# Row gathers, row sizes and weight preparation re-placed in the block stage of a Fourier layer, an expert layer and a SoLU layer

## The chip, the cores and the metric

One core of one Trainium2 chip runs the whole program in one launch. The metric is device time in microseconds (us), the median of several executions. Engines by their names in the profile: PE (matmul), ACT, DVE and POOL (elementwise work; POOL also issues the row gathers, the row scatters and some weight loads), SP (issues the other transfers).

## The reference, cut to what matters

Three layers in a row, all in float32:

```python
X = rfft(x, axis=1)                      # x: 8 x 3072 x 256
Yr, Yi = softshrink(Xr@w_r - Xi@w_i + b_r), softshrink(Xr@w_i + Xi@w_r + b_i)   # lam 0.01
x = irfft(Yr + 1j*Yi).reshape(24576, 256)

e = argmax(x @ w_gate); gate = softmax(x @ w_gate)[e]      # 8 experts
# the first 768 rows of each expert, in row order, are kept; the others give zero rows
y = gate * (relu(x @ w1[e]) @ w2[e])                        # 256 -> 1024 -> 256

h = y @ w_in                                                # 256 -> 1024
s = h * softmax(h)
out = ((s - mean(s)) / sqrt(var(s) + 1e-6) * g_ln) @ w_out  # 1024 -> 256
```

With these inputs every expert has its 768 rows within the first 3 of the 8 batches, so the kernel transforms 3 batches and runs the rest only if a count says otherwise (a branch at the end that is not taken here).

## The kernel before, in words

**Three batches, then sixteen blocks.** Each batch passes a Fourier stage in 12 units (the loop `units`, which calls `middle(u)` after each unit) and an inverse stage (`tail`) that stores rows to `ydram` in HBM and writes down, for every expert, which rows it keeps. Then each expert's 768 places are worked off as 2 blocks of 384 rows (3 tiles of 128 rows), in the order of experts 0, 1, 1, 0, 2, 2, 3, 3, ... 7, 7. I number these blocks 0 to 15. Two slots hold an expert's prepared weights, one for the even experts and one for the odd ones.

**One block.** *gather* (L830): POOL issues 3 indirect DMAs that fetch 3 x 128 rows into one of two row buffers. *words* (L834 to L849): ACT squares each row tile with a sum (L841), DVE makes a power-of-two scale of it (L842, L786 to L788), ACT and DVE split the rows into a high and a low float16 part (L846, L847), and SP issues one DMA transpose of them (L848). *up* U0 to U3 (L873): 12 matmuls each, relu on ACT (L875) and the low part on DVE (L876). *down* D0 to D3 (L888 to L891): 12 matmuls each, which need the relu of the up of the same number. *finish* F (L900 to L909). Then, mixed into the next block: *hidden* H0 to H2 (L925 to L966), one per row tile, with the second layer's first matmul, an exponential (L934) and moments; *norm* N (L972 to L977, on POOL); *halves* C (L965 to L967), which end in a DMA transpose on SP; and *project* P or Q (L996 to L999) with 24 matmuls that need that transpose and an indirect store to `out` on POOL.

**An expert's weights.** `expert_steps` returns steps: four chunks of 512 KB are fetched (L648, L650; chunks 0 and 1 on POOL's queue, 2 and 3 on SP's, in the block stage), each chunk is squared and summed on ACT (`size`, L653, 1.2 us), a pair of sums is added by two one-column matmuls on PE (L659) and made a scale (`scale`), and each half chunk is split on ACT (L674, 0.7 us) and DVE (L675, 0.75 us) (`part`). The second layer's first weight has the same in `first_steps` (L736, L739, L747, L748). Chunks 2 and 3 are the second half of the expert's weights, which the down matmuls read.

**What sets the order.** `run_blocks` writes the program of each block from a list of letters: `ORDER_0` for block 0, `ORDER_1` for block 1, `ORDER` for the others. G is the gather of the next block, X its *words*, E takes the next weight step of the list `side[n]` of this block; steps left over after the last letter follow behind F. What is written is not yet what runs: a planner of the framework lays out each engine's queue from its own estimate of times. It takes an instruction as soon as the inputs and the buffer are there by its estimate, and of several the one that was written first; each engine then runs its queue strictly in that order. The only fences are `pinned()` and `issue_after`: every weight step E is queued behind the last ACT and the last DVE instruction written before it, and `PIN_X = (2,)` does that to the *words* written in block 2 (those of block 3).

**Weight steps before.** 11 steps: all four fetches; two squares and their scale; two squares and their scale; 8 parts. For an expert whose first block is n, the first 5 stand in block n-2 and, after an empty one, 6 in block n-1, which has 5 letters E (so two parts fall behind F). For expert 2 all 11 stand in block 3. Expert 0's own steps are taken in the last batch's units 6 to 11, two a unit, and the 5 steps of `first_steps` (four squares with their matmuls, then 4 parts) in units 7 and 8.

Of the kernel before, what the change touches and what calls it, by code (L numbers as in the profile page):

```python
# [30 lines left out]
GATHER = 9  # L31


ORDER_0 = 'E R U0 L E R U1 E R E D0 R U2 E R E E R D1 E R U3 E R D2 R G E X D3 E E F'.split()

DRAIN = 'I0 I1 S0 M0 I2 B1 T0 S1 M1 B2 T1 S2 M2 T2 P0 P2 P1'.split()
LATER = 8
PIN_X = (2,)
ORDER_1 = 'E U0 H0 U1 D0 E H1 N0 U2 E D1 C0 E G H2 N1 U3 C1 P0 E N2 C2 X D2 D3 F'.split()
BEHIND = ()  # L40
ORDER = 'E Q1 U0 H0 D0 G U1 E Q2 N0 H1 D1 U2 E C0 E H2 N1 C1 X U3 D2 P0 E N2 C2 D3 F'.split()
ROUTE = ((-2, -6), (-2, -6), (-2, -5))
NCH = 8
COUNT = 3
# [83 lines left out]
def _body(tc, x, w_r, w_i, b_r, b_i, w_gate, w1, w2, w_in, w_out, g_ln, cap, con, out):  # L128
# [15 lines left out]
    with sp as sb, dp as dr, pp as ps:  # L144
# [495 lines left out]
        def expert_steps(e, o, load=(dma,) * 4):  # L640

            flat = lambda c: v(o_st + 1024 * c, 1024)
            squares = v(o_flag + 4, 4)

            def fetch(c):
                k = c % 2
                if c < 2:
                    load[c](out=flat(c), in_=w1[bass.ds(e, 1), 128 * k : 128 * k + 128, :].rearrange("o p f -> (o p) f"))  # L648
                else:
                    load[c](out=v3(o_st + 1024 * c, 4, D), in_=w2[bass.ds(e, 1), 512 * k : 512 * k + 512, :].rearrange("o (c p) d -> (o p) c d", p=128))  # L650

            def size(c):
                act(v(o_xr + 1536, 1024), flat(c), ACTF.Square, accum_out=squares[:, c : c + 1])  # L653

            def scale(m):
                p = psum("psc")
                for k in range(2):
                    c = 2 * m + k
                    mm(p[:, 0:1], ones16, squares[:, c : c + 1].bitcast(BF16)[:, 1:2], start=k == 0, stop=k == 1)  # L659
                total = squares[:, 2 * m : 2 * m + 1]  # L660
                vec.tensor_scalar(total, p[:, 0:1], 1e-36, None, ALU.max)
                scales(*weight_scales(o)[m], total, 10)

            def part(c, r):
                h1, l1, h2, l2 = expert_views(o)
                k = c % 2
                if c < 2:
                    at = slice(512 * r, 512 * r + 512)
                    h, l, src = h1[:, k, at], l1[:, k, at], flat(c)[:, at]
                else:  # L670
                    at = slice(4 * k + 2 * r, 4 * k + 2 * r + 2)
                    h, l, src = h2[:, at], l2[:, at], v3(o_st + 1024 * c, 4, D)[:, 2 * r : 2 * r + 2]
                w = weight_scales(o)[c // 2][0]
                act(h, src, ACTF.Copy, scale=w)  # L674
                vec.scalar_tensor_tensor(l, src, w, h, ALU.mult, ALU.subtract)  # L675

            def load_all():
                for c in range(4):
                    fetch(c)

            def half_sized(m):
                size(2 * m)
                size(2 * m + 1)
                scale(m)

            return [load_all] + [lambda m=m: half_sized(m) for m in range(2)] + [lambda c=c, r=r: part(c, r) for c in range(4) for r in range(2)]

        behind = []

# [40 lines left out]
        def first_steps():  # L730

            part_of = lambda a, n: a[:, n // 2, 512 * (n % 2) : 512 * (n % 2) + 512]

            def size():
                for n in range(4):
                    act(v(o_xr, 512), part_of(wi, n), ACTF.Square, accum_out=v(o_flag + 4 + n, 1))  # L736
                p = psum("psc")
                for n in range(4):
                    mm(p[:, 0:1], ones16, v(o_flag + 4 + n, 1).bitcast(BF16)[:, 1:2], start=n == 0, stop=n == 3)  # L739
                total = v(o_flag + 4, 1)  # L740
                vec.tensor_scalar(total, p[:, 0:1], 1e-36, None, ALU.max)
                scales(*i_scale, total, 10)
                vec.tensor_scalar(i_scale[1], i_scale[1], float(2**DOWN), None, ALU.mult)

            def part(n):
                h, l, src = part_of(wi_h, n), part_of(wi_l, n), part_of(wi, n)
                act(h, src, ACTF.Copy, scale=i_scale[0])  # L747
                vec.scalar_tensor_tensor(l, src, i_scale[0], h, ALU.mult, ALU.subtract)  # L748

            return [size] + [lambda n=n: part(n) for n in range(4)]  # L750

        o_w16 = (o_wsb, o_ht + 5120)
        last_weights = lambda: tuple(v(o, 1024).bitcast(F16).rearrange("p (f d) -> p f d", f=8) for o in o_w16)
# [47 lines left out]
        class Block:  # L801
# [23 lines left out]
            def gather(self):  # L825
# [3 lines left out]
                for i in range(NTT):  # L829
                    pool.indirect_dma_start(out=v(o_xg + D * (NTT * self.par + i), D), out_offset=None, in_=ydram[0 : self.rows, :],  # L830
                                            in_offset=bass.IndirectOffsetOnAxis(ap=self.slots(i, 0), axis=0),
                                            bounds_check=self.rows - 1, oob_is_err=False)

            def words(self):  # L834

                at = o_sx + 16 * self.par
                square, power, back = (v(at + 4 * i, NTT) for i in range(3))
                a = f16(o_xr + 768 * self.par, 4).rearrange("p (h k) (i c) -> p h i k c", h=2, i=NTT)
                rows = [v(o_xg + D * (NTT * self.par + i), D) for i in range(NTT)]
                for i in range(NTT):  # L840
                    act(v(o_xr + 2560, D), rows[i], ACTF.Square, accum_out=square[:, i : i + 1])  # L841
                vec.tensor_scalar(square, square, 1e-36, None, ALU.max)  # L842
                scales(power, back, square, 6)
                for i in range(NTT):
                    src, s = rows[i].rearrange("p (k c) -> p k c", k=2), power[:, i : i + 1]
                    act(a[:, 0, i], src, ACTF.Copy, scale=s)  # L846
                    vec.scalar_tensor_tensor(a[:, 1, i], src, s, a[:, 0, i], ALU.mult, ALU.subtract)  # L847
                dma(out=f16(o_ga + 768 * self.par, 4).rearrange("p a (i c) -> p (a i) c", c=128),  # L848
                    in_=v(o_xr + 768 * self.par, 768).bitcast(F16), transpose=True)  # L849
# [199 lines left out]
        def in_order(strict):  # L1049
            return pinned() if strict else ExitStack()  # L1050
# [80 lines left out]
        def run_blocks(blocks, side, free=None, marks=()):  # L1131
# [8 lines left out]
            for n in range(len(blocks)):  # L1140
# [11 lines left out]
                for what in (ORDER_0, ORDER_1, ORDER)[min(n, 2)]:  # L1152
                    i = int(what[1:] or 0)
                    if what[0] == "E":
                        extra()
                    elif what[0] == "U":
                        bl("up")(i)
                    elif what[0] == "D":
                        bl("down")(i)
                    elif what[0] == "R":  # L1160
                        if n == 0 and marks:
                            marks.pop(0)()
                    elif what[0] == "G":
                        of(n + 1, "gather")()
                    elif what[0] == "H":
                        pr("hidden")(i)
                    elif what[0] == "N":
                        if n > 0 and i in BEHIND:
                            with tc.issue_after(blocks[n - 1].exped):
                                pr("norm")(i)  # L1170
                        else:
                            pr("norm")(i)
                    elif what[0] == "C":
                        pr("halves")(i)
                    elif what[0] == "P" and not late:
                        pr("project")(i)
                    elif what[0] == "Q":
                        of(n - 2, "project")(i)
                    elif what[0] == "X":
                        with in_order(n in PIN_X):  # L1180
                            of(n + 1, "words")()
                    elif what[0] == "F":
                        bl("finish")()
                        if late:
                            pr("project")(0)
# [44 lines left out]
        blocks = [Block(e, e * capp + k * BLK, n, where[e], rows, own=n if n < 2 else None) for n, (e, k, rows) in enumerate(plan)]  # L1230
        side = {n: [] for n in range(len(plan))}
        for i, e in enumerate(rest):
            owner = ([EARLY[1], EARLY[0]] + rest)[i]
            first = max(n for n, o in enumerate(order) if o == owner) + 1
            steps = expert_steps(e, where[e], [pool.dma_start] * 2 + [dma] * 2)
            if first + 1 < order.index(e):
                side[first] += steps[:5]
                side[first + 1] += [lambda: None] + steps[5:]
            else:
                side[first] += steps  # L1240

        early = expert_steps(EARLY[0], slot_a)
        load_c2(0, 8)
# [26 lines left out]
        for b in range(FIRST):  # L1270
# [32 lines left out]
            def before_last(b=b, last=last, steps=steps):  # L1303
# [2 lines left out]
                renew(o_hn)  # L1306
                if last:
                    renew(o_ga)
                    blocks[0].words()
                    sums.extend(column_sums())  # L1310
                    sums.pop(0)()
                else:
                    begin(x[b + 1])
# [40 lines left out]
        with tc.If(more > 0):  # L1354
# [24 lines left out]
            with tc.For_i(0, NE, 1) as e:  # L1379
# [5 lines left out]
                    vec.tensor_copy(dst.bitcast(I32) if f < 2 else dst, src[:, bass.ds(e * n, n)])  # L1385
                again = [Block(e, 0, k, slot_a, NT, False, k) for k in range(nblk)]
                again[0].gather()
                again[0].words()
                renew(o_hn)
                run_blocks(again, {})  # L1390
# [26 lines left out]
```

## Time and profile before

| what | value |
|---|---|
| median of 3 runs | 948.74 us (947.61 to 949.88) |
| the profiled execution's own time | 949.85 us |
| its span, first to last instruction | 948.0 us |
| PE busy | 847.8 us (89%) |
| DVE, ACT, POOL busy | 638.2, 481.9, 287.7 us |
| mean granted PE clock | 0.956 |

A busy PE is one with a matmul in its pipeline; at half the clock the same matmuls look twice as long. The idle time in front of an instruction is printed in brackets, with what ended it. The first block's F stands at 358.3 us, the last one's at 913.2 us. All times within the trace are counted from the span's start.

### The profile page before, as it was taken

To read this page: it belongs to the slowest core of one execution; us is meant where nothing else is said; L and a number is where in the kernel's file an instruction comes from. 1 tells how busy PE (TensorE), PEld (TensorE's weight loads), DVE (VectorE), ACT (ScalarE), POOL (GpSimd) and SP (SyncE) were. 2 spreads that over 40 slices of the span, in tenths; PEclk is the share of its full clock that TensorE was granted. 3 is DMA by queue.
4 is the path that set the end of the run, shared out by engine and by line. 5 is a ranking of instruction groups with operands and counts; after the bars stand their busy time and mean duration, and the time that the engine had idled before them with its cause. 6 is when DMAs were issued, how large, how long until landed. Compare 5 with 4: busy or idle time off the path is not lost. (4 is left out here: it accounts for less than half of the span.)

```text
span 948.0 us, 16083 instructions
## 1 busy us (share of the span) xinstructions
PE 847.8 (89%) x5844; PEld 571.4 (60%) x5844; DVE 638.2 (67%) x1640; ACT 481.9 (51%) x848; POOL 287.7 (30%) x450
## 2 busy tenths in 40 slices
PE   8799999999978999796887979788798898899996
PEld 3797479945967465563544645455455565566656
DVE  1475589757976678584765857466575786687674
ACT  2343344333474547375755656365465664565443
POOL 2000000000002044546445344452444434334435
PEclk9899999999979999997989999889898999999999
DMA  8899659975993421534364253362544445432330
GB/s 225 283 287 287 207 165 286 285 249 174 294 301 94 119 81 60 109 84 104 80 151 112 49 136 78 79 148 46 112 83 112 95 80 133 74 67 63 56 79 32
DMA packets 211273, 131.74 MB, mean 139 GB/s; under 512 B 126390, under 2 KB 193331, under 8 KB 211056
## 3 DMA queue, kind: packets, MB, share of 16 engines
q1 hardware_dynamic: 204448, 110.91, 45.9%
q0 software_dynamic: 6736, 19.71, 7.3%
q8 instruction: 48, 0.79, 0.3%
q14 instruction: 41, 0.34, 0.1%
HBM read 50.37 MB, written 50.33 MB: 106 GB/s over the span
## 5 line engine op out<-in xcount | busy, mean ns | idle before, releaser
L996 PE MATMUL pso<-r,r 128*128 128x256 f16 (+1 forms) x792 | 145.1, 286 | 23.0 <-DMA r<-r 22.5
L873 PE MATMUL psH<-r,r 128*128 128x384 f16 x768 | 139.1, 332 | 0.7 <-DVE r L675 0.5
L996 PEld LDWEIGHTS <-r 128*128 128x128 f16 x1080 | 108.7, 102 | 48.4 <-DMA r<-r 26.8
L433 PE MATMUL psm<-r,r 128*128 128x256 f32 x864 | 116.0, 291 | 5.1 <-DVE r L404 3.5
L433 PEld LDWEIGHTS psm<-r,r 128*128 128x128 f32 x864 | 108.8, 196 | 6.1 <-DVE r L404 3.9
L873 PEld LDWEIGHTS <-r 128*128 128x128 f16 x768 | 76.2, 100 | 54.8 <-issue 4.8
L942 DVE SCALAR_TENSOR_TENSOR r<-psh,r 128x1024 f32<-128x1024 f32 x48 | 58.8, 1224 | 48.6 <-ACT r L934 48.4
L888 PE MATMUL psY<-r,r 128*128 128x384 f16 x256 | 55.3, 340 | 40.3 <-ACT r L875 40.3
L830 POOL DMA_INDIRECT r<-ydram,r x48 | 55.3, 1151 | 108.9 <-DVE r L615 61.3
L996 PE MATMUL pso<-r 128*128 128x256 f16 x360 | 87.9, 287 | 0.0
L891 PE MATMUL psY<-r,r 128*128 128x384 f16 x256 | 86.0, 337 | 1.0 <-DVE r L876 0.9
L972 POOL TENSOR_SCALAR r<-r 128x1 f32<-128x1 f32 x48 | 16.2, 338 | 231.6 <-ACT r L952 173.0
L890 PE MATMUL psY<-r,r 128*128 128x384 f16 x256 | 86.3, 338 | 0.0
L875 ACT ACTIVATE r<-psH 128x768 f16<-128x768 f32 x64 | 51.5, 805 | 67.7 <-PE psH L873 65.2
L934 ACT ACTIVATE r<-psh,r 128x1024 f32<-128x1024 f32 x36 | 43.3, 1202 | 69.6 <-DVE r L933 38.9
L876 DVE SCALAR_TENSOR_TENSOR r<-psH,r 128x768 f16<-128x768 f32 x64 | 61.0, 954 | 18.0 <-ACT r L875 17.3
L926 PE MATMUL psh<-r,r 128*128 128x512 f16 x192 | 72.7, 379 | 0.0
L925 PE MATMUL psh<-r,r 128*128 128x512 f16 x192 | 72.7, 379 | 0.0
L932 DVE TENSOR_REDUCE r<-psh 128x1 f32<-128x1024 f32 x48 | 58.5, 1219 | 14.5 <-PE psh L928 14.2
L999 POOL DMA_INDIRECT out<-r x48 | 54.2, 1128 | 31.5 <-DVE r L998 17.9
L966 DVE SCALAR_TENSOR_TENSOR r<-r 128x1024 f16<-128x1024 f32 x36 | 47.6, 1321 | 24.0 <-ACT r L965 22.8
L518 POOL DMA_DIRECT2D r<-c_tok x3 | 1.8, 601 | 200.9 <-DVE r L556 200.4
(212 smaller groups left out, 1663.0 us busy)
## 6 DMA issues: line engine op xcount, KB each, us to landing
out<-r SPq DMA_DIRECT2D x48, 512.0 KB, 6.1
r<-moe_w SPq DMA_DIRECT2D x20, 512.0 KB, 5.0
r<-x SPq DMA_DIRECT2D x24, 384.0 KB, 8.0
r<-gdram SPq DMA_DIRECT2D x36, 256.0 KB, 5.3
ydram<-r SPq DMA_DIRECT2D x36, 192.0 KB, 2.2
r<-moe_w POOLq DMA_DIRECT2D x12, 512.0 KB
gdram<-r SPq DMA_DIRECT2D x12, 384.0 KB, 3.4
ydram<-r SPq DMA_DIRECT2D x36, 64.0 KB, 2.4
```

What stands on the lines that cost most here:

```text
L433: mm(p3[:, gi], a, b, start=i == 0, stop=i == len(seq) - 1)
L830: pool.indirect_dma_start(out=v(o_xg + D * (NTT * self.par + i), D), out_offset=None, in_=ydram[0 : self.rows, :], in_offset=bass.Indirect ...
L873: mm(p3[:, fi, 0:BLK], a, b, start=i == 0, stop=i == 5)
L876: vec.scalar_tensor_tensor(hl_, p3[:, :, 0:BLK], 0.0, hh, ALU.max, ALU.subtract)
L888: mm(y3[:, d, 0:BLK], b, hh[:, fi], start=f == 0, stop=False)
L890: mm(y3[:, d, 0:BLK], a, hh[:, fi], start=False, stop=False)
L891: mm(y3[:, d, 0:BLK], a, hl_[:, fi], start=False, stop=f == 7)
L925: mm(o, a, r, start=k == 0, stop=False)
L926: mm(o, a, w, start=False, stop=False)
L932: vec.tensor_reduce(c(0), p, AX.X, ALU.max, negate=True)
L942: vec.scalar_tensor_tensor(t, p, 1.0, e, ALU.mult, ALU.mult, accum_out=c(3))
L996: mm(p[:, 0:D], a, b, start=n == 0, stop=n == 23)
```

## The change

*words* becomes two functions: `sizes` (the squares and scales, letter X) and `words` (split and transpose, letter Z). A letter K writes the gather for the block after next. `PIN_X` goes. In `ORDER` G is gone and K stands behind P0; X moves from behind C1 to behind U1, and Z stands behind D1. In `ORDER_1` G moves ahead of U2, X behind U3, Z behind C2, and K stands ahead of F. An expert's steps are regrouped into ten (below), five in block n-2 and five in block n-1, for all experts alike. `first_steps` becomes 12 steps: two pairs of squares, three empty steps, the matmuls with the scale, two empty steps, 4 parts; its sums move to places of their own.

```diff
-ORDER_1 = 'E U0 H0 U1 D0 E H1 N0 U2 E D1 C0 E G H2 N1 U3 C1 P0 E N2 C2 X D2 D3 F'.split()
+ORDER_1 = 'E U0 H0 U1 D0 E H1 N0 G U2 E D1 C0 E H2 N1 U3 X C1 P0 E N2 C2 Z D2 D3 K F'.split()
-ORDER = 'E Q1 U0 H0 D0 G U1 E Q2 N0 H1 D1 U2 E C0 E H2 N1 C1 X U3 D2 P0 E N2 C2 D3 F'.split()
+ORDER = 'E Q1 U0 H0 D0 U1 X E Q2 N0 H1 D1 Z U2 E C0 E H2 N1 C1 U3 D2 P0 K E N2 C2 D3 F'.split()
-PIN_X = (2,)
...
-            return [load_all] + [lambda m=m: half_sized(m) for m in range(2)] + [lambda c=c, r=r: part(c, r) for c in range(4) for r in range(2)]
+            groups = [[lambda: fetch(0), lambda: fetch(1)], [lambda: fetch(2), lambda: fetch(3)], [lambda: size(0)], [lambda: size(1)], [lambda: size(2)],
+                      [lambda: scale(0), lambda: size(3)], parts[0:2], [lambda: scale(1), parts[2]], parts[3:6], parts[6:8]]
...
-            return [size] + [lambda n=n: part(n) for n in range(4)]
+            return [lambda: squared(0), lambda: squared(2), wait, wait, wait, size, wait, wait] + [lambda n=n: part(n) for n in range(4)]
...
                     elif what[0] == "X":
-                        with in_order(n in PIN_X):
-                            of(n + 1, "words")()
+                        of(n + 1, "sizes")()
+                    elif what[0] == "Z":
+                        of(n + 1, "words")()
+                    elif what[0] == "K":
+                        of(n + 2, "gather")()
...
+            at = order.index(e)
+            side[at - 2] += steps[:5]
+            side[at - 1] += steps[5:]
```

The arithmetic, the buffers and the counts of instructions of every kind stay as they were.

## Rows read from the trace of the kernel before

**Rows 1.** Busy time per stretch: PE, PEld, DVE, ACT, POOL, clock, DMA.

```profile
589.00:633.30 44.30, 35.09 (x210) 21.52 (x211) 26.36 (x71) 21.34 (x37) 22.69 (x35) 0.89 0.47 107
633.30:670.00 36.70, 33.51 (x205) 20.29 (x204) 25.59 (x71) 22.39 (x40) 11.37 (x17) 0.95 0.40 79
...
854.10:884.10 30.00, 30.00 (x195) 18.85 (x194) 22.31 (x55) 15.86 (x23) 13.16 (x24) 1.00 0.32 67
```

**Rows 2.** Waits from 400 us on: who waited for what, total, times, longest.

```profile
ACT r L841 <- DMA r<-ydram,r: 56.1, 17, 8.1
...
PE psY L888 <- ACT r L875: 40.3, 16, 9.1
...
PE pso L996 <- DMA r<-r: 17.5, 10, 4.3
```

**Rows 3.** ACT in order of time at block 5's start, idle in brackets.

```profile
511.61 0.40 ACT L841 ACTIVATE r<-r 128x256 f32<-128x256 f32 x1
...
519.75 0.42 ACT L841 ACTIVATE r<-r 128x256 f32<-128x256 f32 x1 [7.64 <-DMA r<-ydram,r]
...
520.70 0.79 ACT L875 ACTIVATE r<-psH 128x768 f16<-128x768 f32 x1
```

**Rows 4.** POOL in order of time, same start, then one block later.

```profile
508.45 1.16 POOL L830 DMA_INDIRECT r<-ydram,r  x1 [5.96 <-DVE r L908]
...
513.01 0.63 POOL L648 DMA_DIRECT2D r<-moe_w  x1
...
516.64 1.09 POOL L830 DMA_INDIRECT r<-ydram,r  x1 [0.17 <-issue]
...
542.28 0.65 POOL L648 DMA_DIRECT2D r<-moe_w  x1
```

**Rows 5.** PE in order of time: idle before the first down, and before a project.

```profile
443.54 1.44 PE L888 MATMUL psY<-r,r 128*128 128x384 f16 x4 [9.08 <-ACT r L875]
...
632.15 0.39 PE L996 MATMUL pso<-r,r 128*128 128x256 f16 x1 [4.32 <-DMA r<-r]
...
682.45 1.44 PE L888 MATMUL psY<-r,r 128*128 128x384 f16 x4 [5.18 <-ACT r L875]
```

**Rows 6.** Busy time per stretch around eight waits: first, last, sum.

```profile
434.00:449.50 15.50, 6.42 (x28) 3.56 (x27) 6.16 (x24) 9.77 (x24) 9.12 (x11) 0.67 0.22 62
...
706.00:719.00 13.00, 9.47 (x54) 6.38 (x52) 8.31 (x22) 6.31 (x13) 8.39 (x10) 0.74 0.85 187
sum 94.00, PE 55.35 PEld 32.27 DVE 42.20 ACT 42.47 POOL 46.65; mean PE 6.92 PEld 4.03 DVE 5.27 ACT 5.31 POOL 5.83
```

**Rows 7.** The gathers' and the row squares' lines: first and last start.

```profile
L830 POOL DMA_INDIRECT r<-ydram,r x48: 994/1098/1952, 286.9 to 714.8; - x48
...
L841 ACT ACTIVATE r<-r x48: 399/416/418, 290.6 to 721.0; 128x256 f32<-128x256 f32 x48
```

**Rows 8.** SP in order of time: two transposes of one block.

```profile
532.27 1.79 SPq L967 DMA_TRANSPOSE r<-r  x1
...
542.15 5.39 SPq L967 DMA_TRANSPOSE r<-r  x1
```

**Rows 9.** Busy time per stretch in the last batch, and in block 0.

```profile
262.50:277.80 15.30, 8.96 (x62) 7.93 (x60) 12.19 (x35) 12.71 (x30) 0.00 (x0) 0.80 1.08 321
271.50:282.00 10.50, 7.05 (x35) 6.71 (x35) 7.31 (x22) 9.42 (x20) 0.00 (x0) 0.51 0.89 275
329.80:341.00 11.20, 8.33 (x48) 5.56 (x49) 7.92 (x28) 6.55 (x12) 3.78 (x7) 0.85 0.24 73
```

**Rows 10.** PE in order of time: waits behind weight sizes.

```profile
270.73 0.16 PE L739 MATMUL psc<-r 128*128 128x1 bf16 x1 [1.49 <-ACT r L736]
...
334.85 0.16 PE L659 MATMUL psc<-r 128*128 128x1 bf16 x1 [1.93 <-ACT r L653]
...
657.90 0.81 PE L888 MATMUL psY<-r,r 128*128 128x384 f16 x4 [1.64 <-ACT r L875]
```

**Rows 11.** ACT in order of time: its longest idle time in block 2.

```profile
396.33 0.81 ACT L875 ACTIVATE r<-psH 128x768 f16<-128x768 f32 x1 [7.74 <-PE psH L873]
```

## The prediction on record

> **What bounds the kernel now.** I read the busy time per stretch first. PE is the engine that everything ends on, and in the block stage it runs in two ways. Two neighbouring blocks with weight steps and gathers took 44.3 and 36.7 us, with PE busy 35.1 and 33.5 us of that at a clock of 0.89 and 0.95. A late block without either took 30.0 us with PE busy throughout at 1.00 [rows 1]. The work on PE is the same, so a pair loses some 18 us. DVE is busy 26.4 of 44.3 us, so it is not the bound, nor would it be at 33 us a block (80%).
>
> The waits come second. PE's idle time from 400 us on is nearly all in two lines: 40.3 us in 16 waits of a down matmul for a relu on ACT, and 17.5 us of a project matmul for a transposed half. ACT itself idles 56.1 us in front of the row squares, for gathered rows [rows 2]. The time order shows why these belong together: at block 5's start ACT takes one row square, sits 7.64 us until the next tile has landed, and only then does the relu of U0 [rows 3]. That tile's gather is not waiting for memory: POOL issues the first at 508.45, the third at 516.64, with norm, a scatter and a 512 KB weight fetch in between [rows 4]. PE pays with 9.08 us at 443.54, 5.18 at 682.45 and three like them between (3.49, 4.71, 4.89), 27.4 us in all; three project waits of up to 4.32 us make 11.3 more [rows 5]. Each also costs clock: in the eight stretches around them 0.67 to 0.82 of the pulses were granted, that is at 1.2 GHz for part of the time after the idle, 25.6 us of pulses lost in 94 us. PE was busy 55.4 of these 94, so I count 15 of the 25.6 as lost work [rows 6].
>
> The fact that decides most is in the lines' first and last starts. The last gather, for block 15, is issued at 714.8 and its squares run at 721.0 [rows 7]; block 10 starts there and block 15 some 170 us later. So the planner already runs gathers five to six blocks ahead of use, limited by the two row buffers, wherever the letter G stands.
>
> **Gathers, K, G, X and Z.** No instruction is added or removed: 48 gathers (1.10 us each [rows 7]) and 48 squares stay. In the steady state a row buffer is free when an earlier block's *words* have been read out, and that is set by U3 of the running block, not by a letter. So I give the letters themselves 0 us in blocks 4 to 9, with bounds from a gain of all 54 us (38.6 idle plus 15 of clock) to a loss worked out as rival 3. What moves these waits are three side effects.
>
> (i) Without the pin, *words* of block 3 are no longer held until behind C1 of block 2. Now they are, and the four blocks behind them follow in a burst that ends in the 9.08 us wait in block 3. Set free, the burst falls into blocks 1 and 2, where ACT is idle up to 7.74 us at once [rows 11]. It takes away 9.1 plus 3 of clock (15.5 x 0.33 x 0.59) and costs about one common block start of 5.2 there: a gain of 6.5, bounds -5 and 12.
>
> (ii) At odd starts, E's first step now has a square (1.2 us) and two parts stand in the second E, pinned only to squares of rows that ran blocks ago. Both are written ahead of the far row squares, so by the planner's rule they go first, and the relu of U0 can then come ahead of the last row squares instead of behind them. The fetch at 513.01 also leaves the place between two gathers, since its chunk is read out later. Odd starts other than the burst cost 18.3 us and about 7 of clock; I take a third, 8.5, with bounds 0 and 25.
>
> (iii) A half's transpose took 1.79 us to issue alone and 5.39 when a 512 KB fetch was issued 0.13 us behind it [rows 8, 4]; the project behind such a one waited 4.32 [rows 5]. With two to three parts per E, chunk 1 is free before H2 instead of behind U3, so this fetch starts near C0's transpose, whose project comes two matmul groups later and has slack. 11.3 us and 5 of clock are at stake; I take 7, bounds 0 and 16.
>
> The Trainium skill speaks against (iii): "DMA: Bandwidth & Descriptors", section SWDGE vs HWDGE vs iDMA, says that each DMA engine takes turns between the queues that have work. By it the fetch slows whatever transposes are under way, wherever it is put, and (iii) would be 0, the sum 7 us later. The trace has both a slow and a quick transpose, so I keep 7.
>
> Together 22.
>
> **Weight steps in the blocks.** Counts stay: 4 squares, 2 scales, 8 parts an expert. Now two squares with their scale stand in one E, and the relu behind them is late: the first-down line's other 11 waits, 40.3 - 27.4 = 13 us, are these, 1.64 us the longest [rows 2, 10]. In the change a lone square (1.2 of 2.4 us) stands in an E, and PE's one-column matmuls follow a step later. Halving the delay removes the 0.9 us waits and leaves 0.4 of each 1.64: a gain of 11. Against it the odd blocks take 8 parts instead of 6 or fewer inside the block, three of them in one E (2.1 us of ACT, 2.2 of DVE) ahead of H2's reduce and U3's relu. D3 needs that relu, and D2 and P0 lie between, 5 us of cover. If that cover fails it costs like a pair of squares, up to 1.6 in each of six odd blocks, 10 us. I take 3 and come to 8, bounds 1 and 13. Expert 2's steps spread over two blocks are in this.
>
> The fetches move on POOL's and SP's queues by this too: POOL's norm and scatter queue behind a fetch for 0.65 us, and no matmul waits for these directly, so 0. No wait is added by the regrouping: each scale stands an E behind its squares.
>
> **The last batch and block 0.** In units 7 and 8 four squares alternate with parts on ACT, and PE's one-column matmuls sit in its queue behind each: waits of 1.49, three of 1.06, and four smaller, 6.34 us idle in 15.3 [rows 9, 10]. Then the clock is at 0.51 for 10.5 us with PE busy 7.05, so 3.5 are lost [rows 9]. In the change the matmuls come four steps behind the squares. ACT gets no less to do (12.7 of 15.3 us busy), so I keep 8 of 9.9, bounds 4 and 10. In block 0 the same pairs cost 0.94 and 1.93 idle, and 0.15 of 11.2 us of pulses, 1.7 us [rows 9, 10]: 3.5 of 4.5, bounds 2 and 4.5. The two row-tile sets of blocks 0 and 1 and the drain behind F are untouched: 0.
>
> **Sum.** 22 + 8 + 8 + 3.5 = 41.5. From the profiled execution's 949.85 us that is 908.4; it stands 1.1 above the median of the runs, so 907.
>
> **Rivals.**
>
> 1. *The change does not do what it says: the planner's order around the gathers stays.* For it: rows 7, and equal buffers. Against: the fetches and parts that surround the gathers do move. Then only 8 + 8 + 3.5 count: 929.
>
> 2. *All the waits go.* For it: blocks without far row squares run at 30.0. Against: the third gather of a start cannot land before POOL has issued it, 8 us behind the first. Full prices 54 + 13 + 9.9 + 4.5 = 81: 867.
>
> 3. *Slower: the freed row squares hold ACT at every start.* Place: starts of blocks 1 to 10, which today alternate between a first-down wait and a project wait. If the fetch, the square and the two parts push POOL's and ACT's queues so that each start pays the odd price, 5.2 and 3.4 of clock (last of rows 6: 13.0 x 0.26), that is 86 instead of 54. Less 19.5 for the rest that is 12.5 more: 961. It decides from a mean of 7.4 us a start on. For it: in-order ACT with far work ahead of near work, which nothing in the change forbids, and the pin that held some of it back is gone. Against: the added work is near work.
>
> 4. *The eight parts in the odd block cost their full 10 us while the gathers' waits stay*: 936; it is the upper end of rival 1.
>
> **How the numbers follow.** Forecast 0.48, rivals 1 and 4 0.25, rival 2 0.13, rival 3 0.14. The forecast's own range, from the smaller bounds of (i) to (iii) together with the rest, is 890 to 925. To hold eight in ten it must take in rivals 1 and 4, to 938, and the near half of rival 2, to 880. A measurement of this kernel tells 0.2% from no change, 2 us. Faster 0.83, from all but rival 3 and a piece of rival 4; within that bound 0.04; slower 0.13.
>
> **What would show it.** In the profile after: the wait of L841 for gathered rows falls from 56 us to some 35 (0 by rival 2, unchanged by rival 1); the first-down line's idle from 40 to some 15; the idle at L739 is gone and the stretch from 262 us granted at 1.00; blocks 1 and 2 show a few us more idle, block 3 some 9 less; the transposes of C1 issue in about 2 us. The last row squares still run near block 10's start. I am wrong if the sum of PE's idle in blocks 1 to 10 has not fallen by a third, or if a new line, the reduce of H2 or the relu of U3 in odd blocks, takes its place.

## The result, and the profile after

The changed kernel takes 911.65 us (median of 4 runs, 908.72 to 912.71), beside 949.31 us for the kernel before on the same chip: a ratio of 0.960, 95% interval 0.957 to 0.963. The profiled execution has a span of 910.7 us, where that of before had 948.0: 37.3 us less.

The page's head comes first (busy time, share of the span, instructions). PE is still what everything ends on: it does the same work in a shorter span.

```profile
PE 836.2 (92%) x5844; PEld 566.7 (62%) x5844; DVE 635.1 (70%) x1640; ACT 480.5 (53%) x848; POOL 285.5 (31%) x450
```

To see where the time went I cut both traces at the first instruction of each block's finish (F, on ACT). Differences, after less before, in us: −5.1 up to the first F; then from each F to the next +5.5, +3.3, −11.1, −1.6, −7.8, 0.0, −9.5, +0.9, −9.9, +1.9, −0.2, −4.0, −1.3, +1.5, 0.0; the tail behind the last F is 34.8 in both. So 32.2 came from the blocks, nearly all from the odd ones, and 5.1 from ahead of them.

The same in the stretches from the first F to the eleventh, that is blocks 1 to 10 (columns: length, then busy time of PE, PEld, DVE, ACT, POOL, PE's granted clock, DMA share, GB/s). First the kernel before, then after:

```profile
358.30:751.10 392.80, 334.18 (x2014) 202.73 (x2012) 262.59 (x731) 224.91 (x402) 178.53 (x251) 0.93 0.43 96
```

```profile
353.20:717.70 364.50, 325.84 (x2029) 202.34 (x2028) 259.80 (x725) 222.90 (x400) 175.47 (x255) 0.96 0.46 105
...
387.00:428.10 41.10, 35.22 (x221) 21.83 (x222) 25.71 (x78) 23.94 (x46) 20.29 (x29) 0.96 0.39 85
428.10:462.20 34.10, 31.14 (x204) 19.58 (x203) 26.98 (x73) 22.20 (x40) 17.66 (x26) 1.00 0.54 137
...
572.10:607.00 34.90, 29.72 (x192) 18.30 (x190) 26.97 (x72) 22.04 (x40) 17.62 (x26) 0.99 0.58 135
607.00:644.50 37.50, 36.38 (x224) 23.07 (x225) 24.18 (x69) 21.30 (x38) 17.09 (x25) 0.92 0.37 79
```

PE's idle time in the ten blocks is 58.6 us before (392.8 less 334.2) and 38.7 after, a third less; its busy time fell by 8.3 at a higher granted clock (0.96 for 0.93). The pair that took 44.3 and 36.7 us [rows 1] is now 34.9 and 37.5: the long block became short, and the short one stayed. The even blocks still lose clock: block 8 was granted 0.92.

The waits from 360 us on (who waited for what, total, times, longest) answer to [rows 2]. Those rows count from 400 us on; from 360 us on the first two of their lines are the same, and the project's line of the kernel before is this:

```profile
PE pso L996 <- DMA r<-r: 22.5, 12, 4.3
```

After the change:

```profile
ACT r L838 <- DMA r<-ydram,r: 41.7, 13, 7.2
...
PE pso L998 <- DMA r<-r: 17.3, 8, 4.4
...
PE psY L890 <- ACT r L877: 16.7, 6, 4.6
...
PE psh L927 <- DVE r L955: 6.9, 6, 3.2
```

The down matmul's wait for relu fell from 40.3 us in 16 to 16.7 in 6. The row squares' wait for gathered rows fell only from 56.1 to 41.7. The project's wait for transposed halves fell from 22.5 to 17.3, mostly because two waits in blocks 1 and 2 (1.18 and 3.77) became one of 1.58. A wait of 6.9 us for DVE is new.

ACT in order of time shows the two kinds of block start, against [rows 3]. In the kernel before, block 5 started with this finish of block 4, and the relu of U0 at 520.70 came 11.2 us behind it:

```profile
509.48 0.79 ACT L900 ACTIVATE r<-psY 128x768 f16<-128x768 f32 x1
```

After, no row square stands between finish and relu at an odd start (572.10, block 7) any more: a weight square and two parts, all ready, and the relu of U0 starts 3.0 us behind the finish.

```profile
572.10 0.79 ACT L902 ACTIVATE r<-psY 128x768 f16<-128x768 f32 x1
572.79 1.04 ACT L653 ACTIVATE r<-r 128x1024 f32<-128x1024 f32 x1
...
573.83 1.32 ACT L674 ACTIVATE r<-r,r 128x512 f16<-128x512 f32 x2
575.06 0.79 ACT L877 ACTIVATE r<-psH 128x768 f16<-128x768 f32 x1
...
606.97 0.79 ACT L902 ACTIVATE r<-psY 128x768 f16<-128x768 f32 x1
607.66 1.14 ACT L967 ACTIVATE r<-r 128x1024 f16<-128x1024 f32 x1
615.98 0.42 ACT L838 ACTIVATE r<-r 128x256 f32<-128x256 f32 x1 [7.18 <-DMA r<-ydram,r]
...
617.48 0.79 ACT L877 ACTIVATE r<-psH 128x768 f16<-128x768 f32 x1
```

At the next, even start (606.97) all three squares of a far block's rows, with 7.18 us of waiting, still stand ahead of that relu.

PE in order of time at that start, and its longest waits of the new kinds. The 7.18 us cost the down matmul only 1.10; the project ahead of it had already waited 4.45 for its transposed half:

```profile
380.57 1.20 PE L890 MATMUL psY<-r,r 128*128 128x384 f16 x4 [4.62 <-ACT r L877]
...
407.03 0.39 PE L927 MATMUL psh<-r,r 128*128 128x512 f16 x1 [3.20 <-DVE r L955]
...
606.98 0.39 PE L998 MATMUL pso<-r,r 128*128 128x256 f16 x1 [4.45 <-DMA r<-r]
618.32 0.81 PE L890 MATMUL psY<-r,r 128*128 128x384 f16 x4 [1.10 <-ACT r L877]
```

SP in order of time shows what that half meets (here the float16 halves of a block's second row tile, written at C1). They are transposed behind a weight fetch of SP's own (595.75), one that POOL issues at 596.80 and the transpose of the words (596.25), and take 4.85 us to issue where a lone transpose took 1.79 [rows 8]. Number 7 below tries the fetches.

```profile
595.75 0.39 SPq L650 DMA_DIRECT2D r<-moe_w  x1
596.25 2.61 SPq L850 DMA_TRANSPOSE r<-r  x1
598.96 4.85 SPq L969 DMA_TRANSPOSE r<-r  x1
```

```profile
596.80 0.66 POOL L648 DMA_DIRECT2D r<-moe_w  x1
```

Last, the stretches in front of the blocks, answering to [rows 9], and the row squares' line, to [rows 7]:

```profile
271.50:282.00 10.50, 10.26 (x94) 10.12 (x94) 8.27 (x32) 7.80 (x17) 3.28 (x3) 1.00 0.80 224
289.00:304.00 15.00, 10.57 (x67) 5.34 (x65) 9.87 (x28) 7.85 (x19) 0.00 (x0) 0.77 0.50 125
325.00:335.00 10.00, 7.94 (x44) 5.13 (x43) 6.75 (x18) 3.06 (x5) 3.73 (x7) 0.83 0.27 81
```

```profile
L838 ACT ACTIVATE r<-r x48: 398/416/418, 282.0 to 688.7; 128x256 f32<-128x256 f32 x48
```

PE is busy nearly throughout 271.5 to 282 (it was 7.05 of 10.5 at a clock of 0.51), but it idles later, at 289 to 304 and around 330, and there the clock is lower now. The last row squares run at 688.7, where block 10 has just started (678.8): the planner still runs them five blocks ahead.

### The profile page after: what moved, and what is told of

Read it like the earlier page. It is cut to its first block, busy times and chain, and to the rows that moved or that the text cites. A ratio compares the mean times of both kernels' runs of the same rounds, so it can differ in the third digit from the quotient of the medians.

```text
span 910.7 us, 16080 instructions
## 1 busy us (share of the span) xinstructions
PE 836.2 (92%) x5844; PEld 566.7 (62%) x5844; DVE 635.1 (70%) x1640; ACT 480.5 (53%) x848; POOL 285.5 (31%) x450
## 5 line engine op out<-in xcount | busy, mean ns | idle before, releaser
L998 PE MATMUL pso<-r,r 128*128 128x256 f16 (+1 forms) x792 | 141.1, 281 | 17.8 <-DMA r<-r 17.3
L433 PE MATMUL psm<-r,r 128*128 128x256 f32 x864 | 113.7, 288 | 5.4 <-DVE r L404 3.5
L433 PEld LDWEIGHTS psm<-r,r 128*128 128x128 f32 x864 | 106.6, 192 | 6.5 <-DVE r L404 3.9
L893 PE MATMUL psY<-r,r 128*128 128x384 f16 x256 | 84.5, 331 | 1.5 <-DVE r L878 1.2
L892 PE MATMUL psY<-r,r 128*128 128x384 f16 x256 | 84.6, 331 | 0.0
L927 PE MATMUL psh<-r,r 128*128 128x512 f16 x192 | 73.1, 381 | 7.6 <-DVE r L955 6.9
L974 POOL TENSOR_SCALAR r<-r 128x1 f32<-128x1 f32 x48 | 13.9, 289 | 203.6 <-ACT r L954 127.6
L890 PE MATMUL psY<-r,r 128*128 128x384 f16 x256 | 52.9, 329 | 16.7 <-ACT r L877 16.7
L968 DVE SCALAR_TENSOR_TENSOR r<-r 128x1024 f16<-128x1024 f32 x36 | 47.9, 1330 | 11.5 <-ACT r L967 11.5
```

The source lines that it names most:

```text
L433: mm(p3[:, gi], a, b, start=i == 0, stop=i == len(seq) - 1)
L892: mm(y3[:, d, 0:BLK], a, hh[:, fi], start=False, stop=False)
L893: mm(y3[:, d, 0:BLK], a, hl_[:, fi], start=False, stop=f == 7)
L927: mm(o, a, r, start=k == 0, stop=False)
L998: mm(p[:, 0:D], a, b, start=n == 0, stop=n == 23)
```

## The experiments

The table has each kernel's profiled execution, cut as above: the time up to the first F, the 15 blocks from the first F to the last, and in brackets what each differs from before (us). The sections below read from it. One execution stands for each kernel, and executions differ: the edits of numbers 6 to 10 touch nothing that after has ahead of block 1, and still their first column runs from −3.6 to −7.7. So 2 or 3 us between two rows are not read as an effect.

| kernel | to the first F | blocks | time, ratio [95%] |
|---|---|---|---|
| before | 358.3 | 554.9 | |
| after | 353.2 (−5.1) | 522.7 (−32.2) | 911.65, 0.960 [0.957, 0.963] |
| 1 weight steps alone | 347.8 (−10.5) | 534.1 (−20.8) | 920.95, 0.973 [0.969, 0.977] |
| 2 first_steps alone | 350.6 (−7.8) | 554.3 (−0.6) | 942.79, 0.995 [0.993, 0.998] |
| 3 letters alone | 356.3 (−2.0) | 561.7 (+6.8) | 950.94, 1.004 [1.001, 1.006] |
| 4 after, letters back | 349.1 (−9.3) | 533.9 (−21.0) | 921.74, 0.974 [0.970, 0.978] |
| 5 before, no pin | 358.2 (−0.2) | 552.6 (−2.3) | 944.93, 0.999 [0.996, 1.002] |
| 6 after, sizes pinned from block 1 | 351.9 (−6.4) | 495.5 (−59.4) | 884.14, 0.934 [0.930, 0.938] |
| 7 after, thin fetches | 351.6 (−6.7) | 514.7 (−40.2) | 902.59, 0.952 [0.947, 0.957] |
| 8 after, X ahead of U1 | 354.7 (−3.6) | 534.0 (−20.9) | 923.67, 0.975 [0.970, 0.980] |
| 9 after, sizes pinned from block 2 | 352.3 (−6.1) | 485.8 (−69.1) | 875.12, 0.924 [0.919, 0.928] |
| 10 as 9, words pinned too | 350.6 (−7.7) | 542.4 (−12.5) | 936.06, 0.990 [0.986, 0.993] |
| 11 before, words pinned | 359.6 (+1.2) | 521.8 (−33.1) | 919.31, 0.971 [0.965, 0.976] |
| 12 as 1, words pinned | 349.9 (−8.4) | 552.0 (−2.9) | 933.59, 0.988 [0.984, 0.991] |

In the expectations A is the theory that follows from my reasons (far blocks' row squares hold ACT, and the gain comes from near steps that now go ahead of them), and B its rival; in numbers 1 to 4 B has it that the letters, that is when rows are gathered, sized and split, do the work.

**1 to 4: the parts alone.** Number 1 is the kernel before with the ten weight steps:

```diff
-            return [load_all] + [lambda m=m: half_sized(m) ...
+            groups = [[lambda: fetch(0), lambda: fetch(1)], ...
...
+            side[at - 2] += steps[:5]
+            side[at - 1] += steps[5:]
```

> Before with one part of the change: an expert's ten weight steps over two blocks. Theory A (the weight steps carry the block stage's gain, since they alone change what stands around the gathers): 25 to 30 us below the kernel before, some 920 us; the waits of U0's relu for row squares at odd starts fall below 3 us each. Theory B (the letters and the missing pin carry it): at most the pairs of squares go, 8 to 11 us, some 939. Theory C (parts add up freely): this and the two other parts sum to the whole 37 us.

Number 2 is the kernel before with the twelve first steps alone:

```diff
-            return [size] + [lambda n=n: part(n) for n in range(4)]
+            return [lambda: squared(0), lambda: squared(2), wait, wait, wait, size, wait, wait] + [lambda n=n: part(n) for n in range(4)]
```

> Before with one part of the change: first_steps in twelve steps with its squares apart from its matmuls. Theory A and B alike: the idle at the one-column matmuls in the last batch goes, 5 us of gain (the trace of after has the first F 5.1 us earlier, with block 0's steps in that too), some 944; if the ACT work only moves, 0 to 2 us.

Number 3 has the new letters, X and Z as functions of their own, and no pin, with the old weight steps. The new letters include `ORDER_0`, in which X is followed by E and Z, and one of the two E ahead of F goes. Number 4 is after with the letters of all three orders where they were:

```diff
-ORDER = 'E Q1 U0 H0 D0 U1 X E Q2 N0 H1 D1 Z U2 E C0 E H2 N1 C1 U3 D2 P0 K E N2 C2 D3 F'.split()
+ORDER = 'E Q1 U0 H0 D0 G U1 E Q2 N0 H1 D1 U2 E C0 E H2 N1 C1 X Z U3 D2 P0 E N2 C2 D3 F'.split()
```

> Before with the rest of the change: the orders with K, X and Z, sizes and words apart, no pin; weight steps and first_steps as before. Theory A: the burst moves from block 3 to blocks 1 and 2 and little else, 3 to 8 us of gain, some 943; first-down waits of 4 to 5 us stay at odd starts 5, 7 and 9. Theory B: 20 us or more of gain, below 930, with those waits gone.

> After with the letters put back: the gather one block ahead, sizes and words together where they stood before, still no pin. The planner's queues differ from after's on ACT and DVE. Theory A: within 5 us of after, 907 to 917. Theory B: back up by 15 us or more, above 925.

The weight steps alone take 20.8 us out of the blocks and 10.5 out of the lead, where they also regroup the first experts' weights. The first steps take 7.8 from the same lead. Together with the letters they give 5.1 there, so these two don't add up. In the blocks theory C fails the other way: the three parts by themselves come to 14.6 us (20.8 and 0.6 gained, 6.8 lost), the whole to 32.2. The waits of number 1 (L835, L882, L990 are the squares, the down matmul and the project there) show that the weight steps by themselves shorten ACT's wait for rows and PE's wait for ACT:

```profile
ACT r L835 <- DMA r<-ydram,r: 35.9, 12, 7.0
...
PE psY L882 <- ACT r L869: 19.3, 4, 6.1
PE pso L990 <- DMA r<-r: 18.5, 9, 3.8
```

They free the odd starts from block 5 on by themselves: at block 7's the relu of U0 starts 2.8 us behind the finish, without any part ahead of it.

```profile
570.96 0.79 ACT L894 ACTIVATE r<-psY 128x768 f16<-128x768 f32 x1
...
573.78 0.81 ACT L869 ACTIVATE r<-psH 128x768 f16<-128x768 f32 x1 [0.99 <-PE psH L867]
```

Number 3 missed both expectations. The letters alone gain nothing: the median lies 2.7 us above that of before, and the blocks of the profiled execution, which at 954.86 us lies 3.9 above its median, took 6.8 more. The gathers' wait falls a little, the down matmul's (L893 there) does not, and ACT gets a wait for weight chunks (L653) that the kernel before does not have at all from 360 us on.

```profile
ACT r L841 <- DMA r<-ydram,r: 47.3, 20, 6.1
PE psY L893 <- ACT r L880: 41.5, 15, 6.1
...
ACT r L653 <- DMA r<-moe_w: 32.3, 9, 5.3
```

Number 4 has the blocks of number 1 to 0.2 us (533.9 and 534.1). It missed A, which had it within 5 us of after, and B, which had it above 925. So on top of the weight steps the letters do bring something, 11.2 us in the blocks; number 8 shows which letter.

**5: the pin.** The kernel before with `PIN_X = ()`.

> Before with one edit: the words of block 3 are no longer pinned in block 2. Theory A (the pin only places the burst): block 3's stretch falls by about 9 us, blocks 1 and 2 together rise by about as much, the whole within 3 us of before. Theory B (my step (i)): the rise is only 2 to 4 us, the whole 5 to 7 us faster.

The first stretches changed by +7.3, +0.8 and −8.7: the burst of far squares moved from block 3 to block 1 and cost there what it gave back. Whatever it brings is within the measurement.

**6: far row squares fenced.** The sizes of the next block's rows are held in their place in the program, from block 1 on.

```diff
-                        of(n + 1, "sizes")()
+                        with in_order(n > 0):
+                            of(n + 1, "sizes")()
```

> After with the row sizes (letter X) pinned behind the last ACT and DVE instruction written before them, from block 1 on, so that far blocks' squares cannot stand in ACT's queue ahead of near work. Theory A (far squares ahead of near relus are what is left of the stall): ACT's wait for gathered rows falls from 41.7 us to under 5, some 895 to 903. Theory B (the project's wait for transposes is what binds now): within 3 us of after, 909 to 914. It could also cost if the pins delay near work: above 914.

The gathers' wait is gone altogether and 27 us with it, more than A expected. One wait is new: in block 2, U0 waits for its own transposed rows, since these are now late there.

```profile
391.15 4.02 PE L875 MATMUL psH<-r,r 128*128 128x384 f16 x12 [7.25 <-DMA r<-r]
```

**7: thin fetches.** The weights of experts 2 to 7 are fetched in 1/16 of their columns (so those experts compute with the rest of their buffers as they lie); all instructions stay.

```diff
-load[c](out=flat(c), in_=w1[...].rearrange("o p f -> (o p) f"))
+load[c](out=flat(c)[:, 0:n], in_=w1[..., 0:n].rearrange("o p f -> (o p) f"))
```

> After with the weight fetches of experts 2 to 7 cut to a sixteenth of their columns (32 KB each instead of 512; the rest of these weights is left as it was, so these experts' rows are not computed from their own weights). PE's queue is the same. Theory A (the project waits come from transposes that share the DMA engines with a fetch): project waits fall from 17.3 us to under 5 and transposes that took over 4 us to issue are gone; 898 to 904. Theory B (they come from the order of ACT and SP): project waits stay above 12 us, 909 to 914.

```profile
ACT r L838 <- DMA r<-ydram,r: 41.4, 15, 7.3
...
PE psY L890 <- ACT r L877: 25.3, 6, 5.4
...
PE pso L998 <- DMA r<-r: 4.0, 3, 2.0
```

The project's wait falls from 17.3 to 4.0 us, and no half's transpose takes over 3.40 us to issue. The gathers' wait stays at 41.4, so it is not the fetches' size that makes rows late. Net 9 us: part of the project's 13 comes back as a longer wait of the down matmul (16.7 to 25.3), which, I take it, the project's wait had covered.

**8: X ahead of U1.** One letter of after is moved.

```diff
-ORDER = 'E Q1 U0 H0 D0 U1 X E Q2 ...
+ORDER = 'E Q1 U0 H0 D0 X U1 E Q2 ...
```

> After with one pair of letters exchanged: X ahead of U1 instead of behind it, so that the E behind them is pinned to U1's relu and not to row squares that ran blocks before. Theory A (the two parts freed by that lead the relu of U0 past the row squares, my step (ii)): back to the run with the letters put back, 918 to 923, with first-down waits of 5 us again at every other start. Theory B (the letters gain elsewhere): within 3 us of after.

```profile
ACT r L838 <- DMA r<-ydram,r: 46.4, 16, 7.6
...
PE psY L890 <- ACT r L877: 25.9, 6, 5.8
```

It costs 12 us, and its blocks take as long as those of numbers 4 and 1 (534.0). At the start of block 7 the two parts now run 8 us behind the relu of U0 instead of ahead of it. The relu itself is no later for that:

```profile
578.51 0.79 ACT L902 ACTIVATE r<-psY 128x768 f16<-128x768 f32 x1
...
581.38 0.81 ACT L877 ACTIVATE r<-psH 128x768 f16<-128x768 f32 x1 [1.05 <-PE psH L875]
...
589.71 1.32 ACT L674 ACTIVATE r<-r,r 128x512 f16<-128x512 f32 x2
```

How long the relu of U0 starts behind the finish (us), at three odd and three even starts:

| kernel | blocks 5, 7, 9 | blocks 4, 6, 8 |
|---|---|---|
| before | 11.2, 11.4, 11.6 | 5.4, 7.2, 5.8 |
| 1 weight steps alone | 3.5, 2.8, 2.9 | 10.0, 11.4, 11.0 |
| 8 after, X ahead of U1 | 3.3, 2.9, 2.9 | 11.2, 11.9, 11.7 |
| after | 3.3, 3.0, 2.9 | 9.5, 10.1, 10.5 |
| 9 after, sizes pinned from block 2 | 3.6, 3.6, 3.6 | 5.7, 4.3, 5.3 |

So it is the weight steps that free the odd starts, and with them the far squares go to the even ones. What the place of X brings beside that, 11.3 us, lies mostly in even blocks: without it blocks 4, 6 and 8 take 1.8, 3.2 and 2.4 us longer. In after E follows X and not U1, so its parts are tied to squares that ran blocks ago and go ahead of the relu. That this is what quickens the even blocks is not shown: the exchange also moves X itself. No run moves G and K alone, but X by itself costs all that number 4 loses (11.3 and 11.2 us), which leaves nothing for them there.

**9 and 10: the fence from block 2 on.** Number 9 is number 6 with `n > 1`. Number 10 fences the words (Z) in the same way as well.

> After with the row sizes pinned from block 2 on instead of block 1 on. With block 1 pinned, block 2's U0 waited 7.2 us for its transposed rows, and the clock fell behind it. Theory A (that wait is the pin's only price): 7 to 10 us below the run pinned from block 1, 874 to 878. Theory B (unpinned, the rows of block 3 hold ACT again in block 1): 884 to 890.

> The same with words (letter Z) pinned as well from block 2 on. Theory A (only squares waiting for a gather hold ACT; a split of rows that are there costs nobody): within 2 us of the run with sizes pinned alone. Theory B: the transpose L850 is issued later or the pins delay near work, 3 to 8 us slower.

Number 9 is the fastest kernel here, 36.5 us below after. Two blocks of it, its two largest waits on PE, and the squares' line, which now ends inside block 14 (from 777.2), one block ahead of its rows' use:

```profile
546.90:579.60 32.70, 30.38 (x197) 18.90 (x194) 27.25 (x75) 21.86 (x40) 15.93 (x23) 1.00 0.65 134
579.60:612.70 33.10, 32.55 (x218) 21.16 (x219) 23.58 (x66) 21.35 (x38) 16.85 (x29) 1.00 0.46 100
```

```profile
PE psY L890 <- ACT r L877: 11.1, 6, 2.2
...
PE pso L998 <- DMA r<-r: 7.2, 7, 1.7
```

```profile
L838 ACT ACTIVATE r<-r x48: 398/404/417, 281.7 to 792.2; 128x256 f32<-128x256 f32 x48
```

Both kinds of block take some 33 us at a clock of 1.00. The project's wait fell too, from 17.3 to 7.2, though its fetches keep their size.

Number 10 missed both expectations by far: 61 us worse than number 9. The project's wait for transposed halves rose from 7.2 to 35.9 us, and comes once a block:

```profile
PE pso L998 <- DMA r<-r: 35.9, 14, 6.0
```

The words' transposes do not hold the halves' back in SP's strict order: at the longest of these waits (6.03 us, at 600.65) SP had been free since 590.75, and it issues the half's transpose at 591.96, 0.07 us after DVE ended the low half (L968). On DVE the words' split (L849) and two weight parts (L675) stand ahead of that. Whether these make the half late was not tried.

**11 and 12: the fence without the change, and with the weight steps alone.** Number 11 is the kernel before with its own pin set in all blocks from 2 on (`PIN_X = tuple(range(2, 16))`); number 12 is number 1 with the same.

> Before with one edit: words pinned in all blocks from 2 on, not in block 2 alone. Theory A (far row squares ahead of near relus cause the gathers' waits, whatever the letters): ACT's wait for gathered rows falls from 56 us to under 8; the first-down and project waits at block starts, 38.6 us, and their clock go: 895 to 908, below after. Theory B (the letters of the change are needed for that): above 920.

> Before with the ten weight steps and the same pins (no split of words into two letters, no gather letter, no change of first_steps). Theory A: it lies above the run with sizes pinned from block 2 by first_steps' 5.5 us and up to 5 more for words standing in one piece behind C1: 880 to 888. Theory B (sizes and words apart matter once pinned): above 892.

```profile
PE psY L888 <- ACT r L875: 15.2, 12, 1.6
PE psH L873 <- DMA r<-r: 14.9, 8, 4.7
PE pso L996 <- DMA r<-r: 12.8, 7, 3.7
```

In number 11 (above) one constant brings 3.0%, where the whole change brought 4.0; in the blocks the two are alike (33.1 and 32.2 us). The gathers' wait goes from 56.1 us to none. It falls 11 short of what A expected, and U0 has a new wait of 14.9 us for its transposed rows (L873). In number 12 that wait decides:

```profile
PE psH L867 <- DMA r<-r: 45.9, 7, 9.2
```

So the weight steps, which gain 20.8 us in the blocks of the kernel before, cost 25 to 30 under this fence (552.0 against 521.8 in number 11, but number 12's profiled execution lies 5 us above its median); why the transposed rows come later with them no run shows. And the new places of the letters matter most once the far squares are fenced: sizes early and words free give 875, one piece behind C1 gives 934, of which first_steps account for some 5. There theory B holds.

## Why the prediction came out right, and where its steps did not

Forecast 41.5 us of gain, measured 37.3 in the profiled execution, with 30 forecast in the blocks and 32.2 measured there, 11.5 ahead of them and 5.1 measured. The sum is better than its terms, and that is luck: (i) and (iii) brought little, the weight steps far more than their price, the part ahead of the blocks less than half.

**The letters themselves, 0.** Right for G and K as far as the runs tell. Wrong for X: its place relative to E is worth 11 to 12 us (numbers 4 and 8). I had this under (ii), as a side effect.

**(i) The missing pin, 6.5: failed.** I priced a common start of 5.2 for the place where the burst falls; in number 5 it costs 8.1 there (+7.3, +0.8) for 8.7 given back. In after the first stretches differ by +5.5, +3.3, −11.1 and −1.6: −3.9 together. (My own figures, 12.1 less 5.2, make 6.9.)

**(ii) Odd starts, 8.5: the effect came, but not by the step I gave.** The relu of U0 does come ahead of the far squares, as [rows 3] against the start at 572.10 shows, and at every odd start rather than at a third of them: the odd stretches from block 5 on lost 7.8, 9.5 and 9.9 us. I put this down to two parts that go ahead of the far squares. In numbers 1 and 8 these parts run behind the relu, and it starts as early. So the regrouped weight steps do it; whether by the lone square in the first E, by the fetch that leaves its place between two gathers or otherwise, the runs do not separate. The 18.3 us that I priced also hold 3.49 us of an even start (484.66, block 4).

**(iii) Transposes, 7: failed.** The three waits that I priced at 11.3 us are 10.2 in after (3.11, 4.45 and 2.64, at 534.41, 606.98 and 677.58). I said that chunk 1's fetch would move to C0's transpose; the trace after has two fetches just ahead of C1's instead, and 4.85 us to issue it. Number 7 shows 9 us at stake. The turn-taking that the Trainium skill tells of ("DMA: Bandwidth & Descriptors", SWDGE vs HWDGE vs iDMA) gave 0 for this term, and 1.1 us came; number 7 agrees, since thinner fetches alone quicken the transposes. But "wherever it is put" goes too far: in number 9, with fetches of the old size, C1's transpose in block 7 is issued in 3.13 us (575.22) and its project waits 1.11 (580.15).

**Weight steps, 8: mis-sized.** 20.8 us alone in the blocks. The pairs of squares are gone, as foreseen (six waits left of 16), and the cover of H2's reduce failed only for 6.9 us of L927. The surplus is at the odd starts, which I had counted under (ii): in number 1 the stretches of blocks 5, 7 and 9 lose 7.3, 8.9 and 7.6 us, and those of blocks 6, 8 and 10 grow by 2.8, 2.9 and 3.5.

**The last batch and block 0, 11.5: half.** Alone, first_steps brought 7.8 of the 8 that I gave it (number 2). In after the idle behind weight sizes is gone and 262 to 282 runs at 1.00. But PE then meets its next limits earlier: 3.09 us at 294.28 behind DVE's L442 and 2.06 at 328.99 behind POOL's L582, with clocks of 0.77 and 0.83 around them. I named no next limit for this step.

**The signs.** PE's idle time in blocks 1 to 10 fell by 34%, just over the third that I asked for. C1's transposes were to issue in about 2 us; in the odd blocks from 3 to 11 they take 3.55 to 4.85. A slip that nothing else rests on: the pair of blocks in [rows 1] loses 21 us against two late blocks (81.0 less 60.0), not 18.

**The rivals.** Rival 4's cost of eight parts did not come. Rival 1 was right that the planner still runs gathers and squares five blocks ahead. Rival 3's mechanism, far squares that hold ACT, is real and is what is left: it still stands at every even start from block 2 to block 10, and fencing it (number 9) brings another 36.5 us. It did not make the change slower because the odd starts are free of it.

Open: by which step the regrouped weights free the odd starts; how the place of X quickens the even blocks; why the letters alone make ACT wait for weight chunks; why the two edits ahead of the first F take back some of each other; and what delays the halves in number 10.

## What to carry to other kernels

Where a planner may pull work ahead as far as buffers allow, a letter's place in the program says little by itself; ask what each step is tied to, and what in-order engine it will hold when its data are late. Fence the far consumer that waits for a DMA, and try each fence by itself: here fencing sizes gave 36.5 us, and fencing words too lost 61. When a change is a bundle, run the parts and cut each trace at the same landmarks, block by block: here equal sums (534 us three times) did not say where an edit acts, and the distance from finish to relu did.

## What was not expected of the hardware

How much a transpose slows by what moves beside it: 1.79 us to issue one alone [rows 8], 4.85 behind two fetches, and at most 3.40 with fetches cut to 1/16. And idle time costs PE twice: from 606.1, near the end of the 4.45 us idle ahead of 606.98, to 613 the granted clock is 0.51, which is the lower level (1.2 GHz), while PE is busy 6.03 of these 6.90 us. With such waits gone, number 9 has all its 15 stretches at 1.00 but one (block 5, 0.95).
